# Normalised linear attention with a two-product channel mix: batch 0's first tile handled alone

## The chip, the cores and the metric

The kernel runs on one core of a Trainium2 chip. The metric is device time in microseconds (us). Engines are named as in the profile: PE (TensorE, matmuls), PEld (its weight loads), DVE (VectorE), ACT (ScalarE), POOL (GpSimd, which issues most loads here) and SP (SyncE, which issues the stores).

## The reference

```python
kv  = einsum('bhsd,bhse->bhde', k, v)              # q, k, v: 8 x 8 x 576 x 64
o   = einsum('bhsd,bhde->bhse', q, kv)
x   = o / sqrt(mean(o*o, -1) + 1e-6) * g_norm      # per head, then heads side by side: 8 x 576 x 512
xn  = (x - mean(x)) / sqrt(var(x) + 1e-6) * g_ln   # over the 512
out = x + relu(xn @ w_ch1) @ w_ch2                 # 512 -> 2048 -> 512
```

## The kernel before, in words

A batch has 576 rows; they are worked as four tiles of 128 rows and a remainder of 64, and the remainders of two batches share a tile. For a batch: kv per head pair on PE, q turned (so that d lies on the partitions), then for each tile `o` (q times kv, four matmuls), squares on ACT (`sq`), sums on DVE (`red`), the root on ACT (`root`), its reciprocal on DVE (`inv`), and x from it. `xc` is x less its mean, times g_ln, in bf16; it is turned (`turn`, or `half_turn`/`halves_turn` for 256 columns at a time) into `xT`. The first product (`mm1`, L402) multiplies w1 with `xT`, and ACT takes it through relu (L405); the second (`mm2`, `mm2_part`, L418) multiplies with w2; `finish` (L423) scales by 1/std, adds x and stores.

There are two ways to x. Later tiles use `y` and `x` (two DVE passes over o: times the reciprocal, times g_norm). Batch 0's tiles 0 and 1 use `o_g` and `x_g`: four more matmuls with kv already times g_norm (`kv_g`), and one DVE pass.

The order is written by hand. Every group of 16 matmuls of the first product, and every four of the second, calls `tick()`, which first runs what the agenda holds for that slot (`at(slot, fn)`). Each engine executes its instructions in the order in which they were recorded, so what is recorded earlier on an engine stands ahead. PSUM buffers come from the pools `ps_m` (1), `ps_out` (2), `ps1` (3) and `ps2` (2).

Batch 0 is the start-up, and the place of the change. k comes by the SP and ACT queues, everything else by POOL's: v in two halves, q's lower rows in two halves of the heads, w1's first quarter, q's upper rows, the rest of w1, w2, then batch 1. PE first runs 18 filling matmuls on zeros (`fill`, L196; nobody reads their result). `kv_first` makes kv for two head pairs at a time and copies it to `kv_pack` and, times g_norm, to `kv_g`. Then tiles 0 and 1 go together, by halves of the heads: `half_turn` turns q of both tiles, `half_o` makes o and its squares, `half_red` the sums. Filling matmuls stand in the waits. Tile 0's `xT` is turned before the first product starts; tile 1's, q of tiles 2 and 3 and of the remainder (`turn_first`) and tiles 2 and 3 are on the agenda. The first product of batch 0 runs tile by tile, columns 0 to 8 of tile 0 (in units of 128, four to a group), then 0 to 8 of tile 1, and so on; its second product accumulates the first 8 of 16 for all four tiles, then 8 more for each, and finishes each.

Lines: kv's matmuls L219, their copies L222 and L223, times g_norm L224 and L225; q's turn L183, its copy L191 (tiles 2, 3, remainder) or L492 (tiles 0, 1); o L500 (by halves) and L260, squares L502 and L266, sums L506 and L287, root L297, reciprocal L304; `o_g` L272, `x_g` L278; `xc` by halves L532, its turn L541 and copy L542, whole L321, turn L337 and copy L339; q of batch 1 regrouped L590.

Of the kernel before, what the change touches and what calls it, by code (L numbers as in the profile page):

```python
# [14 lines left out]
def kernel(  # L15
# [11 lines left out]
    nc = tc.nc  # L27
    f32 = mybir.dt.float32
    bf16 = mybir.dt.bfloat16
# [56 lines left out]
    def lo(t, b, h0=0, h1=H):  # L86
        return t[b, h0:h1, :S_LO, :].rearrange("h (p j) d -> p h j d", j=JJ)
# [29 lines left out]
    def pairs(t, hp0, hp1):  # L117
        return bass.AP(tensor=t.tensor, offset=t.offset + hp0 * 2 * S * D,
                       ap=[[JP * D, 128], [2 * S * D, hp1 - hp0], [1, JP * D]])
# [3 lines left out]
    nc.vector.memset(fill_sb, 0.0)  # L123
    nc.sync.dma_start(k_f[:, :HP // 2], pairs(k, 0, HP // 2))
    nc.scalar.dma_start(k_f[:, HP // 2:], pairs(k, HP // 2, HP))
    nc.gpsimd.dma_start(v_p[:, :HP // 2], pairs(v, 0, HP // 2))  # L126
    nc.gpsimd.dma_start(v_p[:, HP // 2:], pairs(v, HP // 2, HP))
    for h0 in (0, H // 2):
        nc.gpsimd.dma_start(q_in[0][:64, h0:h0 + H // 2], lo(q, 0, h0, h0 + H // 2))
    load_w1(0)  # L130
    make_identity(nc, identity)
    nc.gpsimd.dma_start(q_in[0][64:, :, :J], up(q, 0))
# [44 lines left out]
    def turn_groups(tp, i, h0, h1):  # L177
        groups = ((0, 2 * i), (0, 2 * i + 1)) if i < 2 else ((64, 2 * i - 4), (64, 2 * i - 3))
        if i == J:
            groups = ((0, J),)  # L180
        for h in range(h0, h1):
            for half, (p0, j) in enumerate(groups):
                nc.tensor.transpose(  # L183
                    tp[h % 2 * D:h % 2 * D + D, (h - h0) // 2, half * 64:half * 64 + 64],
                    q_in[0][p0:p0 + 64, h, j, :], identity[p0:p0 + 64, p0:p0 + 64])
        return 64 * len(groups)

    def turn_first(i, pool, tag, copy=nc.scalar.copy):
        tp = pool.tile([128, HP, 128], bf16, tag=tag, name="tp")
        n = turn_groups(tp, i, 0, H)  # L190
        copy(qts[0][:, i, :, :n], tp[:, :, :n])  # L191

    def fill(n, pool=ps2, tag="p2"):
        for _ in range(n):
            p1 = pool.tile([128, 512], f32, tag=tag, name="p1")
            nc.tensor.matmul(p1, lhsT=fill_sb[:, :128], rhs=fill_sb, start=True, stop=True)  # L196
            del p1

    def turn_q_dma(b):
        q_p = kv_in.tile([128, JJ, H, D], bf16, tag="qp", bufs=2)  # L200
# [3 lines left out]
            q_t.rearrange("p j hp t -> p (j hp) t"), q_p.rearrange("p j h d -> p (j h d)"))  # L204
        qts[b] = q_t

    def kv_first():
        kvp = held[0] = kv_pack[0]
        g = g_norm_sb.to_broadcast([128, HP // 2, D])
        for i, (pe, te, po, to) in enumerate(((ps_m, "misc", ps1, "p1"), (ps1, "p1", ps1, "p1"))):  # L210
            even = pe.tile([128, HP // 2, D], f32, tag=te, name="even")
            odd = po.tile([128, HP // 2, D], f32, tag=to, name="odd")
            hps = slice(i * HP // 2, (i + 1) * HP // 2)
            for hp in range(hps.start, hps.stop):
                for j in range(JP):
                    js = slice(j * D, (j + 1) * D)
                    for hh, dst in ((0, even), (1, odd)):
                        rows = slice(hh * D, hh * D + D)
                        nc.tensor.matmul(dst[rows, hp - hps.start, :], lhsT=k_p[rows, hp, js],  # L219
                                         rhs=v_p[rows, hp, js],  # L220
                                         start=(j == 0), stop=(j == JP - 1))
            nc.vector.tensor_copy(kvp[:D, hps, :D], even[:D])  # L222
            nc.scalar.copy(kvp[D:, hps, D:], odd[D:])  # L223
            nc.vector.tensor_mul(kv_g[:D, hps, :D], even[:D], g[:D])  # L224
            nc.vector.tensor_mul(kv_g[D:, hps, D:], odd[D:], g[D:])  # L225
            del even, odd

    def kv_of(b):
        kv_ps = ps_m.tile([128, HP, D], f32, tag="misc", name="kv_ps")
# [114 lines left out]
    def main_tile(b, j, pool=None, tag="ops"):  # L344
        q_t, kvp = qts[b], held[b]
        if b not in blks:
            blks[b] = new_block("main", 3)
        return Tile([(slice(0, 128), lambda hp: q_t[:, j, hp, :], kvp)], blks[b], j, pool, tag)
# [109 lines left out]
    def at(slot, fn):  # L458
        agenda.setdefault(int(slot), []).append((slot, fn))
# [12 lines left out]
    del gl_row  # L472

    qts[0] = qt_pool.tile([128, JJ, HP, 128], bf16, tag="qt", name="qt")
    fill(18)
    kv_first()


    t = [main_tile(0, i, ps2, "p2") for i in range(4)]
    for i in range(2):  # L480
        t[i].ss = work.tile([128, H, 1], f32, tag="ss", bufs=4, name="ss")
    sqs = [work.tile([128, H, D], f32, tag="sq", name="sq") for _ in range(2)]
    banks = (((ps_out, "ops"), (ps_m, "misc")), ((ps_out, "ops"), (ps1, "p1")))
    copies = ((nc.scalar.copy, nc.scalar.copy), (nc.vector.tensor_copy, nc.vector.tensor_copy))

    def half_turn(half):
        hp0 = half * HP // 2
        tps = [ps2.tile([128, HP // 2, 128], bf16, tag="p2", name="tp") for _ in range(2)]
        for i in range(2):
            turn_groups(tps[i], i, 2 * hp0, 2 * hp0 + H // 2)  # L490
        for i in range(2):
            copies[half][i](qts[0][:, i, hp0:hp0 + HP // 2], tps[i])  # L492

    def half_o(i, half):
        hp0 = half * HP // 2
        pool, tag = banks[half][i]
        o = pool.tile([128, H // 2, D], f32, tag=tag, name="o_half")
        flat = o.rearrange("p h e -> p (h e)")
        for k2 in range(HP // 2):
            nc.tensor.matmul(flat[:, k2 * 128:(k2 + 1) * 128], lhsT=qts[0][:, i, hp0 + k2, :],  # L500
                             rhs=kv_pack[0][:, hp0 + k2, :], start=True, stop=True)
        nc.scalar.activation(sqs[i][:, half * H // 2:(half + 1) * H // 2], o, func=AF.Square)  # L502

    def half_red(i, half):
        hs = slice(half * H // 2, (half + 1) * H // 2)
        nc.vector.tensor_reduce(t[i].ss[:, hs], sqs[i][:, hs], axis=AX.X, op=ALU.add)  # L506

    half_turn(0)
    fill(2, ps_out, "ops")
    half_o(0, 0)  # L510
    half_turn(1)
    half_o(1, 0)
    half_o(0, 1)
    half_red(0, 0)
    half_red(0, 1)
    half_o(1, 1)
    t[0].root()
    half_red(1, 0)
    half_red(1, 1)
    t[0].o_g(ps1, "p1")  # L520
    t[1].o_g(ps1, "p1")
    fill(8)
    t[0].x_g()
    t[1].root()


    def halves_xc(i):
        x_blk, st, _ = t[i].blk
        for c in range(2):
            cs = slice(c * Dm // 2, (c + 1) * Dm // 2)  # L530
            xc = work.tile([128, Dm // 2], bf16, tag="xch", bufs=4, name="xc")
            nc.vector.scalar_tensor_tensor(xc, in0=x_blk[:, i, cs], scalar=st[:, 1, i:i + 1],  # L532
                                           in1=g_ln_sb[:, cs], op0=ALU.add, op1=ALU.mult)
            yield xc

    def halves_turn(i, xcs, pool, tag):
        xT = t[i].blk[2]
        for c, xc in enumerate(xcs):
            tp = pool.tile([128, 2, 128], bf16, tag=tag, name="tp")
            for kk in range(2):  # L540
                nc.tensor.transpose(tp[:, kk, :], xc[:, kk * 128:(kk + 1) * 128], identity)  # L541
            nc.scalar.copy(xT[:, 2 * c:2 * c + 2, i * 128:(i + 1) * 128], tp)  # L542

    halves_turn(0, halves_xc(0), ps_out, "ops")
    t[1].x_g()
    xc1 = list(halves_xc(1))


    def x2():
        t[2].red()  # L550
        t[2].y()
        t[2].x()
        t[2].xc()

    def x3():
        t[3].sq()
        t[3].red()
        t[3].y()
        t[3].x()
        t[3].xc()  # L560

    def o2():
        t[2].o()
        t[2].sq()

    def next_loads():
        nc.gpsimd.memset(k_in[0][64:, :, J], 0.0)
        nc.gpsimd.memset(v_in[0][64:, :, J], 0.0)
        load_batch(2)

    at(1, lambda: turn_first(2, ps_m, "misc", nc.vector.tensor_copy))
    at(1.1, lambda: halves_turn(1, xc1, ps_out, "ops"))
    at(1.2, o2)
    at(1.3, x2)
    at(4, lambda: turn_first(3, ps_m, "misc"))
    at(5, lambda: t[3].o())
    at(5.1, x3)
    at(6, lambda: t[2].turn(True))
    at(9, lambda: turn_first(J, ps_m, "misc"))
    at(9.5, next_loads)  # L580
    at(10, lambda: t[3].turn(True))
    for i in range(4):
        at(16 + i, lambda i=i: t[i].var())
    at(20, lambda: (rstd_of(0), t.clear()))
# [41 lines left out]
    at(32 * B + 14, lambda: rstd_of("rem"))  # L626


    for ts, c0, c1 in ((0, 0, 8), (1, 0, 8), (0, 8, 12), (1, 8, 12), (0, 12, 16), (1, 12, 16),
                       (2, 0, 16), (3, 0, 16)):  # L630
        mm1(0, ts, 1, c0, c1)
    p2s = [ps1.tile([128, Dm], f32, tag="p1", name="p2") for _ in range(2)]
    p2s += [ps2.tile([128, Dm], f32, tag="p2", name="p2") for _ in range(2)]
    for ts in range(4):
        mm2_part(0, ts, p2s[ts], 0, nDe // 2)
    for ts in range(4):
        p2 = p2s[ts]
        p2s[ts] = None
        mm2_part(0, ts, p2, nDe // 2, nDe)
        finish(0, ts, p2)  # L640
        del p2
    del blks[0], m1s[0]
# [41 lines left out]
```

## Time and profile before

| | |
|---|---|
| median of 5 runs | 291.66 us (291.62 to 291.71) |
| the profiled execution | 291.63 us, of which the span 289.5 us |
| PE busy | 282.0 us, 97% of the span |
| DVE, ACT busy | 151.0 and 155.0 us |
| L402, first product | 1024 matmuls, 131.8 us |
| L418, second product | 608 matmuls, 129.2 us |
| L196, filling matmuls | 28, 8.2 us |
| v's two halves | 288 KB each, 6.5 us from issue to landing (median) |
| q's two lower halves | 160 KB each, 7.0 us |

The span runs from the first to the last instruction of the profiled execution; the device time also holds what lies around it. Loads convert from 4-byte to 2-byte numbers on the way, and sizes are those written. Matmuls are pipelined and their ends are modelled, so the busy time of a stretch says whether PE had something to do, not how fast it went; the distance between starts says that. The page has the span in 40 slices of 7.2 us.

### The profile page before, as it was taken

The page shows a single profiled execution, that of the slowest core. Times are in us where ns is not written, and L with a number is a line of the kernel's source. Part 1 is how long each engine was busy: PE and PEld are TensorE (multiplying, and loading weights), DVE is VectorE, ACT ScalarE, POOL GpSimd, SP SyncE. Part 2 cuts the span into 40 slices and gives each one's busy share as a digit, 9 for nine tenths or more (in the row PEclk, how much of TensorE's full clock was granted, in tenths as well). Part 3 has the DMA queues.
Part 4 walks back from the last instruction along what each step waited for, and adds up shares of the span by engine and source line. Part 5 has one row for each costly group of instructions (what it writes and reads, how often), then busy time and mean ns, then how long its engine had stood idle before and what let it go on. Part 6 is the DMA issues. An engine that isn't in the chain of part 4 may idle for free.

```text
span 289.5 us, 5791 instructions
## 1 busy us (share of the span) xinstructions
PE 282.0 (97%) x2312; PEld 158.7 (55%) x2312; DVE 151.0 (52%) x335; ACT 155.0 (54%) x339; POOL 41.1 (14%) x68
## 2 busy tenths in 40 slices
PE   7889999999999999999999999999999999999995
PEld 3579755995569644445444444444444444444444
DVE  5775028847997783765366925762578300220022
ACT  3467755885469832882189418920894076016500
POOL 8522520032032003200410023000000000000000
PEclk9999999999999999999999999999999999999999
DMA  7999999469899919995997189937302510131033
GB/s 214 203 206 204 198 204 219 109 99 196 149 178 144 165 40 156 209 169 100 144 204 110 41 147 197 175 76 149 69 18 54 112 36 0 39 81 28 0 74 73
DMA packets 64378, 36.10 MB, mean 125 GB/s; under 512 B 31836, under 2 KB 59356, under 8 KB 64352
## 3 DMA queue, kind: packets, MB, share of 16 engines
q0 software_dynamic: 28016, 17.76, 44.2%
q1 hardware_dynamic: 35824, 17.25, 31.1%
q10 hardware_dynamic: 512, 0.72, 0.8%
q8 instruction: 18, 0.29, 0.4%
q14 instruction: 8, 0.07, 0.1%
HBM read 36.71 MB, written 9.44 MB: 159 GB/s over the span
## 4 chain that ended last, share of the span: by engine, by line
PE 93%; DMA 2%; ACT 1%; DVE 1%; issue 1%; POOL 0%; POOLq 0%
PE p L418 43%; PE p L402 43%; PE o_ps L260 3%; DMA v_in<-in_v_dram 2%; PE kv_ps L235 2%; PE tp L183 1%; PE p L196 1%; PE tp L337 1%; ACT sq L266 0%; PE tp L170 0%; DVE xc L532 0%; PE o_half L500 0%; POOL v_in L126 0%; ACT m L405 0%; DVE x_blk L278 0%
## 5 line engine op out<-in xcount | busy, mean ns | idle before, releaser
L402 PE MATMUL p<-xT_blk,w_sb 128*128 128x128 bf16 (+2 forms) x1024 | 131.8, 286 | 0.2
L418 PE MATMUL p<-w_sb,m 128*128 128x512 bf16 (+2 forms) x608 | 129.2, 368 | 0.0
L405 ACT ACTIVATE m<-p 128x512 bf16<-128x512 f32 x144 | 85.5, 596 | 43.3 <-PE p L402 41.1
L402 PEld LDWEIGHTS <-w_sb 128*128 128x128 bf16 x1024 | 78.4, 98 | 44.1 <-issue 0.6
L418 PEld LDWEIGHTS <-m 128*128 128x128 bf16 x608 | 56.8, 98 | 61.7
L423 DVE SCALAR_TENSOR_TENSOR o_sb<-p,rstd,x_blk 128x512 f32<-128x512 f32 (+2 forms) x38 | 27.4, 721 | 54.3 <-PE p L418 51.4
L266 ACT ACTIVATE sq<-o_ps 128x512 f32<-128x512 f32 x34 | 20.2, 595 | 41.5 <-PE o_ps L260 41.4
L287 DVE TENSOR_REDUCE ss<-sq 128x8 f32<-128x512 f32 x34 | 23.0, 678 | 11.2 <-ACT sq L266 11.2
L329 ACT ACTIVATE dev<-x_blk,st_blk 128x512 f32<-128x512 f32 x36 | 25.7, 714 | 4.6 <-DVE st_blk L315 4.4
L321 DVE SCALAR_TENSOR_TENSOR xc<-x_blk,st_blk,g_ln_sb 128x512 bf16<-128x512 f32 x34 | 25.6, 752 | 1.2
L292 DVE TENSOR_TENSOR y<-o_ps,inv 128x512 f32<-128x512 f32 x34 | 23.5, 692 | 3.0
L311 DVE SCALAR_TENSOR_TENSOR x_blk<-y,g_norm_sb 128x512 f32<-128x512 f32 x34 | 23.5, 692 | 1.2
L411 DVE RECIPROCAL rstd<-rstd 128x4 f32<-128x4 f32 x9 | 1.6, 174 | 35.3 <-ACT rstd L410 35.3
L304 DVE RECIPROCAL inv<-rms 128x8 f32<-128x8 f32 x36 | 7.2, 200 | 23.0 <-ACT rms L297 23.0
L98 POOL COPY gate<-qt 1x1 bf16<-1x1 bf16 x5 | 0.9, 177 | 114.1 <-DMA qt<-q_p 114.1
L297 ACT ACTIVATE rms<-ss,eps_sb 128x8 f32<-128x8 f32 x36 | 10.7, 297 | 9.4 <-DVE ss L287 8.7
L260 PEld LDWEIGHTS <-qt 128*128 128x128 bf16 (+1 forms) x152 | 9.9, 100 | 7.4 <-issue 1.7
L260 PE MATMUL o_ps<-kv_pack,qt 128*128 128x128 bf16 (+1 forms) x152 | 13.3, 220 | 0.2 <-DVE qt L191 0.2
L196 PE MATMUL p<-fill_sb 128*128 128x512 bf16 x28 | 8.2, 451 | 1.2 <-DVE eps_sb L137 1.2
L329 ACT ACTIVATION_READ_ACCUMULATOR dev<-x_blk,st_blk 128x1 f32 x36 | 6.9, 191 | 0.0
L238 ACT CAST kv_pack<-kv_ps 64x256 bf16<-64x256 f32 x7 | 2.6, 366 | 7.2 <-PE kv_ps L235 7.2
L235 PEld LDWEIGHTS <-k_in 128*64 128x64 bf16 x280 | 5.0, 112 | 2.6 <-issue 2.5
(79 smaller groups left out, 117.0 us busy)
## 6 DMA issues: line engine op xcount, KB each, us to landing
out_dram<-o_sb SPq DMA_DIRECT2D x70, 128.0 KB, 2.5
w_sb<-in_moe_w_ch_dram POOLq DMA_DIRECT2D x8, 512.0 KB, 13.9
k_in<-in_k_dram POOLq DMA_DIRECT2D x7, 320.0 KB, 6.0
v_in<-in_v_dram POOLq DMA_DIRECT2D x7, 320.0 KB, 9.1
q_in<-in_q_dram POOLq DMA_DIRECT2D x7, 320.0 KB, 13.0
q_in<-in_q_dram POOLq DMA_DIRECT2D x8, 256.0 KB, 12.8
k_in<-in_k_dram POOLq DMA_DIRECT2D x7, 256.0 KB, 6.9
v_in<-in_v_dram POOLq DMA_DIRECT2D x7, 256.0 KB, 11.2
```

The source lines that it names most:

```text
L196: nc.tensor.matmul(p1, lhsT=fill_sb[:, :128], rhs=fill_sb, start=True, stop=True)
L260: nc.tensor.matmul(flat[rows, hp * 128:(hp + 1) * 128], lhsT=lhsT_of(hp), rhs=kvp[:, hp, :], start=True, stop=True)
L266: nc.scalar.activation(self.sq_t, self.o_ps, func=AF.Square)
L287: nc.vector.tensor_reduce(self.ss, self.sq_t, axis=AX.X, op=ALU.add)
L292: nc.vector.tensor_mul(self.y_t, self.o_ps, self.inv().to_broadcast([128, H, D]))
L311: nc.vector.scalar_tensor_tensor(x_blk[:, ts].rearrange("p (h d) -> p h d", h=H), in0=self.y_t, scalar=1.0, in1=g_norm_sb.to_broadcast([12 ...
L321: nc.vector.scalar_tensor_tensor(self.xc_t, in0=x_blk[:, self.ts], scalar=st[:, 1, self.ts:self.ts + 1], in1=g_ln_sb, op0=ALU.add, op1=ALU ...
L329: nc.scalar.activation(dev, x_blk[:, ts], func=AF.Square, bias=st[:, 1, ts:ts + 1], accum_out=st[:, 2, ts:ts + 1])
L402: nc.tensor.matmul(p1[:, i, :], lhsT=w1_sb[:, kk, de * 128:(de + 1) * 128], rhs=blk[2][:, kk, sl], start=(kk == 0), stop=(kk == nK - 1))
L405: nc.scalar.activation(m1[:, de0:de0 + per, sl], p1, func=AF.Relu)
L418: nc.tensor.matmul(p2[:, c0:c1], lhsT=m1s[b][:, de, ts * 128:(ts + 1) * 128], rhs=w2_sb[:, de, c0:c1], start=(de == 0), stop=(de == nDe - 1))
L423: nc.vector.scalar_tensor_tensor(o_sb[:, c0:c1], in0=p2[:, c0:c1], scalar=rstds[b][:, ts:ts + 1], in1=blks[b][0][:, ts, c0:c1], op0=ALU.mu ...
```

## The change

It is confined to batch 0, in six places.

- Loads: v's first three head pairs in one piece, then of q's lower rows the first two of five columns (all that tile 0 needs), then v's last pair, then the rest of q's lower rows. Before: v's two halves, then two halves of q by heads.
- kv in parts of three pairs and of one (`KvFirst`), each with its copies and its products with g_norm placed one by one. Tile 0's q is turned between the two parts, whole.
- Tile 0 alone: its o, squares and sums in two parts (six heads and two). Tile 1's o, squares and sums follow whole, its sums behind tile 0's two `xc` halves; its q, and the remainder's, are turned within the first wait.
- On slot 1 q of tiles 2 and 3 is turned one right behind the other, around them tile 1's `xT` halves (the second one copied by DVE instead of ACT) and tile 2's o; tile 2 takes the way by `o_g` and `x_g`. Tile 3's o is on slot 5 as before, `turn` of tile 2 on 5 instead of 6, of tile 3 on 11 instead of 10.
- The first product of batch 0 runs tiles 0 and 1 by turns, four columns at a time, so that tile 1 is needed by the second group; tile 2's first 12 stand before columns 12 to 16 of all. The second product accumulates 8, 4 and 4 of 16, each for all four tiles, and finishes each in the last round.
- Filling matmuls write one buffer over and over (`fill(n, p1)`) and so don't wait for each other; 18 at the start as before, then 1, 3 and 5 instead of 2 and 8.

```diff
-    nc.gpsimd.dma_start(v_p[:, :HP // 2], pairs(v, 0, HP // 2))
-    nc.gpsimd.dma_start(v_p[:, HP // 2:], pairs(v, HP // 2, HP))
-    for h0 in (0, H // 2):
-        nc.gpsimd.dma_start(q_in[0][:64, h0:h0 + H // 2], lo(q, 0, h0, h0 + H // 2))
+    nc.gpsimd.dma_start(v_p[:, :HP - 1], pairs(v, 0, HP - 1))
+    nc.gpsimd.dma_start(q_in[0][:64, :, :2], lo(q, 0)[:, :, :2])
+    nc.gpsimd.dma_start(v_p[:, HP - 1:], pairs(v, HP - 1, HP))
+    nc.gpsimd.dma_start(q_in[0][:64, :, 2:], lo(q, 0)[:, :, 2:])
...
+    kv_a = KvFirst(0, HP - 1, ((ps_m, "misc"), (ps1, "p1")))
+    kv_b = KvFirst(HP - 1, HP, ((ps1, "p1"), (ps1, "p1")))
...
+    kv_a.mms()
+    kv_a.copies()
+    turn_first(0, ps2, "p2")
+    kv_a.times_g()
+    fill(1)
+    kv_b.mms()
+    kv_b.copies()
+    part_o(kv_a)
+    part_o(kv_b)
+    part_sq(kv_a)
+    part_sq(kv_b)
+    kv_b.times_g()
+    part_red(kv_a)
+    part_red(kv_b)
+    turn_first(1, ps_m, "misc")
     t[0].root()
-    half_red(1, 0)
-    half_red(1, 1)
-    t[0].o_g(ps1, "p1")
+    t[0].o_g(ps2, "p2")
+    dead = fill(3)
+    t[1].o()
+    t[1].sq()
+    turn_first(J, ps_m, "misc")
     t[1].o_g(ps1, "p1")
-    fill(8)
+    fill(5, dead)
     t[0].x_g()
-    t[1].root()
...
+    for c, xc in enumerate(halves_xc(0)):
+        half_turn(0, c, xc, nc.scalar.copy)
+    t[1].red()
     t[1].x_g()
     xc1 = list(halves_xc(1))
...
+    def before_1():
+        turn_first(2, ps_m, "misc")
+        tp = ps2.tile([128, HP, 128], bf16, tag="p2", name="tp")
+        turn_groups(tp, 3, 0, H)
+        half_turn(1, 0, xc1[0], nc.scalar.copy)
+        t[2].o()
+        half_turn(1, 1, xc1[1], nc.vector.tensor_copy)
+        t[2].sq()
+        nc.scalar.copy(qts[0][:, 3], tp)
+        t[2].red()
+        t[2].root()
+
+    def before_2():
+        t[2].o_g(ps2, "p2")
+        t[2].x_g()
+        t[2].xc()
+
+    def before_5():
+        t[3].o()
+        t[3].sq()
+        t[3].red()
+        t[3].y()
+        t[3].x()
+        t[3].xc()
...
-    for ts, c0, c1 in ((0, 0, 8), (1, 0, 8), (0, 8, 12), (1, 8, 12), (0, 12, 16), (1, 12, 16),
-                       (2, 0, 16), (3, 0, 16)):
+    for ts, c0, c1 in ((0, 0, 4), (1, 0, 4), (0, 4, 8), (1, 4, 8), (0, 8, 12), (1, 8, 12),
+                       (2, 0, 12), (0, 12, 16), (1, 12, 16), (2, 12, 16), (3, 0, 16)):
         mm1(0, ts, 1, c0, c1)
...
-    for ts in range(4):
-        mm2_part(0, ts, p2s[ts], 0, nDe // 2)
+    for de0, de1 in ((0, nDe // 2), (nDe // 2, nDe * 3 // 4)):
+        for ts in range(4):
+            mm2_part(0, ts, p2s[ts], de0, de1)
     for ts in range(4):
...
-        mm2_part(0, ts, p2, nDe // 2, nDe)
+        mm2_part(0, ts, p2, nDe * 3 // 4, nDe)
         finish(0, ts, p2)
```

More of the change, by code (lines that the diff above doesn't have):

```diff
@@ L191, in turn_first, with fill @@
         copy(qts[0][:, i, :, :n], tp[:, :, :n])
-    def fill(n, pool=ps2, tag="p2"):
+    def fill(n, p1=None):
+        if p1 is None:
+            p1 = ps2.tile([128, 512], f32, tag="p2", name="p1")
         for _ in range(n):
-            p1 = pool.tile([128, 512], f32, tag=tag, name="p1")
             nc.tensor.matmul(p1, lhsT=fill_sb[:, :128], rhs=fill_sb, start=True, stop=True)
-            del p1
+        return p1
     def turn_q_dma(b):
@@ L205, in turn_q_dma, with __init__, mms, copies @@
         qts[b] = q_t
[L207 to L214, printed above, removed]
+    class KvFirst:
+        def __init__(self, hp0, hp1, pools):
+            self.hps, self.pools = slice(hp0, hp1), pools
+        def mms(self):
+            n = self.hps.stop - self.hps.start
+            (pe, te), (po, to) = self.pools
+            self.even = pe.tile([128, n, D], f32, tag=te, name="even")
+            self.odd = po.tile([128, n, D], f32, tag=to, name="odd")
+            for hp in range(self.hps.start, self.hps.stop):
                 for j in range(JP):
                     js = slice(j * D, (j + 1) * D)
-                    for hh, dst in ((0, even), (1, odd)):
+                    for hh, dst in ((0, self.even), (1, self.odd)):
                         rows = slice(hh * D, hh * D + D)
-                        nc.tensor.matmul(dst[rows, hp - hps.start, :], lhsT=k_p[rows, hp, js],
-                                         rhs=v_p[rows, hp, js],
+                        nc.tensor.matmul(dst[rows, hp - self.hps.start, :],
+                                         lhsT=k_p[rows, hp, js], rhs=v_p[rows, hp, js],
                                          start=(j == 0), stop=(j == JP - 1))
[L222 to L226, printed above, removed]
+        def copies(self):
+            nc.vector.tensor_copy(kv_pack[0][:D, self.hps, :D], self.even[:D])
+            nc.scalar.copy(kv_pack[0][D:, self.hps, D:], self.odd[D:])
+        def times_g(self):
+            g = g_norm_sb.to_broadcast([128, self.hps.stop - self.hps.start, D])
+            nc.vector.tensor_mul(kv_g[:D, self.hps, :D], self.even[:D], g[:D])
+            nc.vector.tensor_mul(kv_g[D:, self.hps, D:], self.odd[D:], g[D:])
+            del self.even, self.odd
     def kv_of(b):
@@ L474 @@
     qts[0] = qt_pool.tile([128, JJ, HP, 128], bf16, tag="qt", name="qt")
+    held[0] = kv_pack[0]
     fill(18)
[L476 to L516, printed above, removed]
-    t[0].root()
-    half_red(1, 0)
-    half_red(1, 1)
-    t[0].o_g(ps1, "p1")
+    kv_a = KvFirst(0, HP - 1, ((ps_m, "misc"), (ps1, "p1")))
+    kv_b = KvFirst(HP - 1, HP, ((ps1, "p1"), (ps1, "p1")))
@@ new lines, with part_o @@
+    t = [main_tile(0, 0)] + [main_tile(0, i, *((ps1, "p1") if i == 1 else (ps2, "p2")))
+                             for i in range(1, 4)]
+    t[0].ss = work.tile([128, H, 1], f32, tag="ss", bufs=4, name="ss")
+    sq_0 = work.tile([128, H, D], f32, tag="sq", name="sq")
+    o_0 = {}
+    def part_o(kv_x):
+        hp0, hp1 = kv_x.hps.start, kv_x.hps.stop
+        o_0[hp0] = ps_out.tile([128, 2 * (hp1 - hp0), D], f32, tag="ops", name="o_part")
+        flat = o_0[hp0].rearrange("p h e -> p (h e)")
+        for hp in range(hp0, hp1):
+            nc.tensor.matmul(flat[:, (hp - hp0) * 128:(hp - hp0 + 1) * 128],
+                             lhsT=qts[0][:, 0, hp, :], rhs=kv_pack[0][:, hp, :],
+                             start=True, stop=True)
@@ new lines, in part_sq, with part_red @@
+    def part_sq(kv_x):
+        hp0, hp1 = kv_x.hps.start, kv_x.hps.stop
+        nc.scalar.activation(sq_0[:, 2 * hp0:2 * hp1], o_0.pop(hp0), func=AF.Square)
+    def part_red(kv_x):
+        hs = slice(2 * kv_x.hps.start, 2 * kv_x.hps.stop)
+        nc.vector.tensor_reduce(t[0].ss[:, hs], sq_0[:, hs], axis=AX.X, op=ALU.add)
+    kv_a.mms()
[8 more added lines that the diff above has]
+    part_sq(kv_a)
@@ L521 @@
+    part_sq(kv_b)
[3 more added lines that the diff above has]
+    turn_first(1, ps_m, "misc")
+    t[0].root()
+    t[0].o_g(ps2, "p2")
[3 more added lines that the diff above has]
+    turn_first(J, ps_m, "misc")
     t[1].o_g(ps1, "p1")
-    fill(8)
+    fill(5, dead)
+    del dead
     t[0].x_g()
-    t[1].root()
     def halves_xc(i):
@@ L534, in halves_xc, with half_turn @@
             yield xc
[L536 to L544, printed above, removed]
+    def half_turn(i, c, xc, copy):
+        tp = ps_out.tile([128, 2, 128], bf16, tag="ops", name="tp")
+        for kk in range(2):
+            nc.tensor.transpose(tp[:, kk, :], xc[:, kk * 128:(kk + 1) * 128], identity)
+        copy(t[i].blk[2][:, 2 * c:2 * c + 2, i * 128:(i + 1) * 128], tp)
+    for c, xc in enumerate(halves_xc(0)):
+        half_turn(0, c, xc, nc.scalar.copy)
+    t[1].red()
     t[1].x_g()
     xc1 = list(halves_xc(1))
-    def x2():
-        t[2].red()
-        t[2].y()
-        t[2].x()
+    def before_1():
[7 more added lines that the diff above has]
+        nc.scalar.copy(qts[0][:, 3], tp)
+        t[2].red()
+        t[2].root()
+        del tp, xc1[:]
+    def before_2():
+        t[2].o_g(ps2, "p2")
+        t[2].x_g()
         t[2].xc()
-    def x3():
+    def before_5():
+        t[3].o()
         t[3].sq()
@@ L560, in x3 @@
         t[3].xc()
-    def o2():
-        t[2].o()
-        t[2].sq()
     def next_loads():
@@ L569, in next_loads @@
         load_batch(2)
[L571 to L579, printed above, removed]
+    at(1, before_1)
+    at(2, before_2)
+    at(5, lambda: t[2].turn(True))
+    at(5.1, before_5)
     at(9.5, next_loads)
-    at(10, lambda: t[3].turn(True))
+    at(11, lambda: t[3].turn(True))
     for i in range(4):
```

## The prediction, made before the result was known

> **What bounds the kernel now.** I read the page's span in slices first, then the chain that ended last, then the timeline of each engine from 7 to 34 us, then the landings of the first loads.
>
> ```profile
> PE   7889999999999999999999999999999999999995
> ...
> PEclk9999999999999999999999999999999999999999
> ...
> PE 93%; DMA 2%; ACT 1%; DVE 1%; issue 1%; POOL 0%; POOLq 0%
> ```
>
> TensorE is full but for the first three slices (22 us) and the last, and its granted clock is full throughout. So the time is the moment from which TensorE is fed, plus its work, plus the holes in it. The stretches say where the holes are (columns: length, then busy us with counts for PE, PEld, DVE, ACT, POOL, then clock, DMA share, GB/s):
>
> ```profile
> 8.00:16.00 8.00, 6.23 (x119) 3.65 (x112) 6.37 (x21) 3.86 (x12) 3.58 (x6) 1.00 1.30 203
> ...
> 26.00:34.00 8.00, 8.00 (x140) 7.50 (x137) 1.23 (x4) 5.95 (x13) 4.41 (x7) 1.00 1.38 199
> 34.00:50.00 16.00, 15.94 (x137) 8.31 (x136) 7.06 (x15) 9.58 (x25) 2.42 (x3) 1.00 1.34 207
> ```
>
> The change touches what lies before 33 us, and the order of batch 0's second product. TensorE's timeline there (start, us, operation; L402 is the first product, 16 matmuls a group; L183 turns q, L541 and L337 turn x, L260 is q times kv):
>
> ```profile
> 14.94 0.68 PE L541 MATMUL tp<-identity,xc 128*128 128x128 bf16 x4 [0.84 <-DVE xc L532]
> 15.69 1.34 PE L402 MATMUL p<-xT_blk,w_sb 128*128 128x128 bf16 x16
> 16.96 0.44 PE L183 MATMUL tp<-identity,q_in 64*64 64x64 bf16 x16
> 17.33 0.40 PE L541 MATMUL tp<-identity,xc 128*128 128x128 bf16 x4
> 17.93 0.40 PE L260 MATMUL o_ps<-kv_pack,qt 128*128 128x128 bf16 x4 [0.20 <-DVE qt L191]
> 18.16 2.84 PE L402 MATMUL p<-xT_blk,w_sb 128*128 128x128 bf16 x48
> ...
> 27.92 5.52 PE L402 MATMUL p<-xT_blk,w_sb 128*128 128x128 bf16 x96
> 33.28 1.03 PE L418 MATMUL p<-w_sb,m 128*128 128x512 bf16 x4
> ```
>
> The first group that counts starts at 15.69 and waits for its third matmul until 16.09. From 18.16 on, 15 groups, 24 q transposes, 8 x transposes and 4 o matmuls fill the time to 33.28. Unit prices from these rows: a group 0.893 (96 matmuls run 27.92 to 33.28), 16 q transposes 0.37, four 128-wide matmuls 0.22. Later work is as many matmuls as before, so the forecast is: when does batch 0's second product (L418) start instead of 33.28?
>
> What sets 15.69 is tile 0's chain, on VectorE and ScalarE:
>
> ```profile
> 12.64 0.30 ACT L297 ACTIVATE rms<-ss,eps_sb 128x8 f32<-128x8 f32 x1 [0.21 <-DVE ss L506]
> 13.18 0.19 DVE L304 RECIPROCAL inv<-rms 128x8 f32<-128x8 f32 x1
> 13.48 0.69 DVE L278 SCALAR_TENSOR_TENSOR x_blk<-og_ps,inv 128x512 f32<-128x512 f32 x1
> ```
>
> VectorE is doing tile 1's sums (L506, 12.19 to 13.2) when tile 0's root is ready at 12.94. That is what handling tile 0 alone removes.
>
> **The change, step by step** (estimates of the new kernel in us from the span's start, each from a row of before).
>
> *Loads.* v's halves (288 KB, 256 packets of 1152 bytes each) landed at 7.45 and 8.89, q's halves (160 KB, 256 of 640 bytes) at 9.68 and 10.5. The software queue moved no packet before 5.6, when k was done, and ran without a hole since, so the order of the four issues decides and their issue time (2.9 us together, as before) does not. Price per packet: 1152 bytes 5.6 ns, 1024 bytes 4.9 (w1), 640 bytes 3.2, 512 bytes 2.6 (q's upper rows: 512 packets, 12.95 to 14.29). The new q pieces have 512 packets of 256 and of 384 bytes, which the trace does not show. Bounds: in proportion to bytes 0.67 and 1.0 us; at the 512-byte price 1.34 each. The line through the four rows gives 1.5 and 2.1 ns, so 0.78 and 1.07, which I take. Landings: three pairs of v 7.45 + 0.72 = 8.17; q's first piece 8.95; v's last pair 9.67; rest of q 10.75. Everything behind is 0.25 later: w1's first quarter 13.2 and q's upper rows 15.45, needed at 14.9 and 16.2, so covered; beyond that cover it is one for one.
>
> [...]
>
> *Tile 0.* kv's matmuls follow their landing by 0.08 (rows 0.09, 0.04) and each other by 0.016: 54 from 8.25 to 9.10. Copies begin 0.21 later, as at 8.31 before. The turn of tile 0 starts at 9.12 (its q is there); ScalarE's copy follows at 9.66, behind the kv copy, 0.58 long: 10.24. v's last pair: 18 matmuls 9.75 to 10.03, copied by 10.46, behind VectorE's two products with g. o: 10.33; squares from 10.70 (128x384, 0.49, between the rows for 256 and 512) and 11.12; sums 0.55 and 0.29 wide from 11.26, overlapping 0.09 as the rows do: 12.01. Root 12.04, reciprocal 12.38, x 12.68 against 13.48: **-0.80**. ScalarE's copy of tile 1's q stands ahead of that root: turn at 10.8, copy 11.36 to 11.94, so it just fits.
>
> *First group.* x to third matmul was 13.48 to 16.09; the same 2.61 gives 15.29, and the group ends at 17.03 - 0.80 = 16.23. The nine new filling matmuls (ten before) end at 13.8, and the turn of the 64-row remainder and tile 1's o stand in the same wait, so they cost nothing while x's transpose comes at 14.14.
>
> *Tile 1.* Here time is given back. Its sum now follows both halves of tile 0's xc: 14.42 to 15.11; the root waits for ScalarE's xT copies: 15.18; reciprocal 15.52; x at 15.82 against 15.51. So tile 1 is 0.31 later while tile 0 is 0.80 earlier, and the second group needs tile 1, where before it needed tile 0 alone: the cover is gone. TensorE: q of tiles 2 and 3 (0.74) to 16.97; hole of 0.31 until x's first half (15.82 + 1.46 = 17.28); o of tile 2 at 17.43, behind relu and copy on ScalarE; second half 17.68; ScalarE's xT copy done 17.98, VectorE's (0.28 as L492's) 18.29. Group two: two matmuls at 18.0, the rest from 18.34, to 19.21 (0.87 as in group one). Holes together 0.82.
>
> *From there.* 14 groups 12.50, og of tile 2 0.22 (new; it replaces one VectorE pass of 0.69), x of tiles 2 and 3 and o of tile 3 0.66. One hole: tile 3's root stands on ScalarE ahead of a relu, and the fourth group behind needs that buffer: 0.1, where before lost 0.3 to the same at 25.4. Sum 13.48: the second product begins at 32.69, against 33.28: **-0.59**.
>
> *Second product in 8, 4, 4 instead of 8, 8.* Same matmuls. Its four finishes move together behind ticks 28 to 31. VectorE runs nearly without a hole from 44.3 to 57.2 there; it ends tile (1,2)'s xc at 55.87 and TensorE takes it at 56.96. I get 56.1 in the new order: cost nothing by 0.3 to 0.8; without that cover, one for one.
>
> The profiled execution was 291.63 (span 289.5 and 2.1 around it; the median of five is 291.66). 291.63 - 0.59 = **291.0**.
>
> [...]
>
> **Rivals.**
> 1. *More gain.* If tile 1's chain is a few tenths earlier than my row sums, the holes of 0.82 close for the most part: -1.2, 290.4. For: every hole has the same cause. Against: the VectorE order is fixed, its durations are rows.
> 2. *The gain goes back.* Tile 1's x at 16.4 instead of 15.82 (its sum or root pushed behind a copy) moves group two one for one: 291.6. For: three engines alternate with no slack there.
> 3. *Slower.* Tile 1's q copy stands ahead of tile 0's root on ScalarE, and the last q piece lands last. Landing later than about 11.0 delays the root one for one (turn, copy and hand-over take 1.04 to the root at 12.04), and q's first piece delays the turn as well. If a packet of 256 or 384 bytes costs what one of 640 does (3.2 ns), the pieces take 1.66 each: turn 0.75 later, rest of q at 12.2, x at 13.95, +0.68: 292.3. The gain is gone from about 2.6 ns a packet on, which is the 512-byte price. Against: the four rows lie on one line.
> 4. *Not as it says.* If v's last pair is late anyway, tile 0 alone waits for it in o; that is inside the sum (VectorE, not the landing, sets 10.46).
>
> **Numbers.** Forecast 0.55, rival 1 0.16, rival 2 (with 4) 0.12, rival 3 0.17. 0.2% is 0.58 us, about what a measurement of this kernel can tell from no change. The forecast lies on that edge: of its 0.55 I give 0.34 to faster. Faster 0.34 + 0.16 = 0.50; within 0.21 + 0.12 = 0.33; slower 0.17. The forecast's own range is 290.7 to 291.4. Range for all 290.3 to 292.3: from rival 1 to rival 3 at the 640-byte price.
>
> **What would show it.** Right: x of tile 0 near 12.7, first group near 14.9, holes before and inside group two, second product near 32.7. Wrong: q's first piece landing after 9.5, tile 0's root waiting for a copy, tile 1's x after 16.4, TensorE waiting for a relu between 22 and 28 or for xc near 57, or a clock below 1.00.

## The result, and the profile after

| | before | after |
|---|---|---|
| median | 291.74 us (50 runs) | 290.92 us (26 runs, 290.78 to 292.71) |
| ratio, 95% interval | | 0.9969 [0.9961, 0.9976] |
| the profiled execution | 291.63 us | 290.97 us |
| its span | 289.5 us | 289.2 us |
| outside the span | 2.13 us | 1.77 us |
| batch 0's second product begins | 33.28 us | 32.98 us |

The kernel is faster by 0.31%, and 291.0 was forecast. The table holds a warning, though: the span became shorter by 0.30 us only, where the prediction had 0.59, and 0.36 us went from a part of the time that the prediction did not speak of. (One of the 26 executions, 292.71, has a mean clock of 0.994; the last section says what that may be.)

Lines of the new kernel: q's turn L183, kv L224, o L502 and L270, `o_g` L282, `x_g` L288, `xc` by halves L546, its turn by halves L553 and whole L347, copies of the whole turn L349, first product L412, relu L415, second product L428, root L307, reciprocal L314, fill L197.

The page of after, its slices (tenths busy) and its chain by engine:

```profile
PE   8889999999999999999999999999999999999995
...
PEclk9999999999999999999999999999999999999999
...
PE 91%; DMA 2%; DVE 2%; ACT 2%; issue 1%; DVEq 0%; POOLq 0%
```

At this scale only the first digit and two points of the chain have changed. The stretches of after (same columns as before):

```profile
8.00:16.00 8.00, 7.24 (x155) 4.87 (x155) 5.67 (x18) 4.37 (x12) 3.75 (x6) 1.00 1.35 202
...
26.00:34.00 8.00, 7.96 (x130) 7.31 (x128) 1.55 (x4) 5.81 (x11) 4.45 (x7) 1.00 1.38 199
```

PE is busy a microsecond more between 8 and 16 us, with 155 matmuls instead of 119, but between 26 and 34 it issues 130 where it issued 140 before. Most of these ten are another mix (before has eight turns of q there, and after is 0.30 further into the second product, whose matmuls are longer), so the count says where to look, not what is lost. The timeline of PE in after (start, us, operation) shows the gain and where it is given back:

```profile
14.20 0.68 PE L553 MATMUL tp<-identity,xc 128*128 128x128 bf16 x4
14.95 1.34 PE L412 MATMUL p<-xT_blk,w_sb 128*128 128x128 bf16 x16
16.21 0.70 PE L183 MATMUL tp<-identity,q_in 64*64 64x64 bf16 x32
17.30 0.28 PE L553 MATMUL tp<-identity,xc 128*128 128x128 bf16 x2 [0.39 <-DVE xc L546]
...
18.05 1.26 PE L412 MATMUL p<-xT_blk,w_sb 128*128 128x128 bf16 x16
19.14 0.39 PE L282 MATMUL og_ps<-kv_g,qt 128*128 128x128 bf16 x4
...
22.49 5.76 PE L412 MATMUL p<-xT_blk,w_sb 128*128 128x128 bf16 x96
28.09 0.39 PE L347 MATMUL tp<-identity,xc 128*128 128x128 bf16 x4
28.31 4.83 PE L412 MATMUL p<-xT_blk,w_sb 128*128 128x128 bf16 x80
32.98 1.24 PE L428 MATMUL p<-w_sb,m 128*128 128x512 bf16 x5
```

The first group ends at 16.21 instead of 17.03: -0.82. Then there is the wait for tile 1 at 17.30, and one inside the second group (16 matmuls in 1.09 between the starts at 18.05 and 19.14, where 0.89 is the price). The two long pieces of the first product take too long as well, and the bracket shows nothing of it, because PE's busy time is modelled through such holes; the distance of starts does: 96 matmuls 22.49 to 28.09 are 5.60 (price 5.36), 80 matmuls 28.31 to 32.98 are 4.67 (price 4.47). What stands in these two, the chain of waits of after tells (start, us, what):

```profile
24.57 0.30 ACT rms L307
24.88 0.49 ACT m L415
...
25.41 2.85 PE p L412 x48
28.29 0.60 ACT m L415
28.88 0.49 ACT xT_blk L349
...
29.41 3.73 PE p L412 x64
```

At 24.57 tile 3's root runs on ScalarE ahead of a relu, and PE waits for the buffer that this relu empties. At 28.88 the copy of tile 3's turned `xc` has had to wait for a relu, and the matmuls that read it start at 29.41: only one group covers the way from turn to copy. The first of these is in the prediction (0.1 was written, 0.24 it is); the second (0.20) is not.

### The profile page after: what moved, and what is told of

It reads as the page before. It is cut to its first block, busy times and chain, and to the rows that moved or that the text cites. A ratio compares the mean times of both kernels' runs of the same rounds, so it can differ in the third digit from the quotient of the medians.

```text
span 289.2 us, 5791 instructions
## 1 busy us (share of the span) xinstructions
PE 282.3 (98%) x2315; PEld 158.9 (55%) x2315; DVE 149.8 (52%) x331; ACT 155.5 (54%) x338; POOL 41.0 (14%) x68
## 4 chain that ended last, share of the span: by engine, by line
PE 91%; DMA 2%; DVE 2%; ACT 2%; issue 1%; DVEq 0%; POOLq 0%
PE p L428 43%; PE p L412 42%; PE o_ps L270 3%; DMA v_in<-in_v_dram 2%; PE kv_ps L245 2%; ACT m L415 1%; DVE x_blk L288 0%; DVE xc L546 0%; PE tp L347 0%; ACT sq L276 0%; ACT xT_blk L349 0%; PE tp L170 0%; ACT rms L307 0%; DVE ss L512 0%; PE odd L224 0%
## 5 line engine op out<-in xcount | busy, mean ns | idle before, releaser
L412 PE MATMUL p<-xT_blk,w_sb 128*128 128x128 bf16 (+2 forms) x1024 | 131.8, 286 | 0.4
L428 PE MATMUL p<-w_sb,m 128*128 128x512 bf16 (+2 forms) x608 | 129.2, 368 | 0.0
L415 ACT ACTIVATE m<-p 128x512 bf16<-128x512 f32 x144 | 85.5, 596 | 43.8 <-PE p L412 41.8
L412 PEld LDWEIGHTS <-w_sb 128*128 128x128 bf16 x1024 | 78.5, 98 | 44.6 <-issue 1.1
L428 PEld LDWEIGHTS <-m 128*128 128x128 bf16 x608 | 56.8, 98 | 61.7
L276 ACT ACTIVATE sq<-o_ps 128x512 f32<-128x512 f32 x35 | 20.8, 596 | 42.1 <-PE o_ps L270 42.1
L297 DVE TENSOR_REDUCE ss<-sq 128x8 f32<-128x512 f32 x35 | 23.7, 678 | 11.4 <-ACT sq L276 11.4
L302 DVE TENSOR_TENSOR y<-o_ps,inv 128x512 f32<-128x512 f32 x33 | 22.8, 692 | 3.0
L321 DVE SCALAR_TENSOR_TENSOR x_blk<-y,g_norm_sb 128x512 f32<-128x512 f32 x33 | 22.8, 692 | 1.1
L314 DVE RECIPROCAL inv<-rms 128x8 f32<-128x8 f32 x36 | 7.2, 201 | 24.8 <-ACT rms L307 24.8
L307 ACT ACTIVATE rms<-ss,eps_sb 128x8 f32<-128x8 f32 x36 | 10.7, 297 | 8.0 <-DVE ss L297 7.7
L270 PEld LDWEIGHTS <-qt 128*128 128x128 bf16 (+1 forms) x156 | 10.2, 100 | 7.3 <-issue 1.7
L270 PE MATMUL o_ps<-kv_pack,qt 128*128 128x128 bf16 (+1 forms) x156 | 13.7, 220 | 0.0
L197 PE MATMUL p<-fill_sb 128*128 128x512 bf16 x27 | 8.5, 467 | 1.2 <-DVE eps_sb L137 1.2
```

What stands on the lines that cost most here:

```text
L270: nc.tensor.matmul(flat[rows, hp * 128:(hp + 1) * 128], lhsT=lhsT_of(hp), rhs=kvp[:, hp, :], start=True, stop=True)
L276: nc.scalar.activation(self.sq_t, self.o_ps, func=AF.Square)
L297: nc.vector.tensor_reduce(self.ss, self.sq_t, axis=AX.X, op=ALU.add)
L302: nc.vector.tensor_mul(self.y_t, self.o_ps, self.inv().to_broadcast([128, H, D]))
L321: nc.vector.scalar_tensor_tensor(x_blk[:, ts].rearrange("p (h d) -> p h d", h=H), in0=self.y_t, scalar=1.0, in1=g_norm_sb.to_broadcast([12 ...
L412: nc.tensor.matmul(p1[:, i, :], lhsT=w1_sb[:, kk, de * 128:(de + 1) * 128], rhs=blk[2][:, kk, sl], start=(kk == 0), stop=(kk == nK - 1))
```

## The experiments

The theory after the result: PE's way through the start-up is the predicted one but for two holes that were sized wrongly or missed, and the 0.36 outside the span is the program's and has nothing to do with it. Its rival on the second point: the time outside is a thing of the chip or the day, and the kernel before would show the smaller value too if it were run beside. On the first point each hole has a rival of its own: that it belongs to something else and stays when its supposed cause is taken away. What each would give is in the expectation of each run. So the kernel before was run again, and parts of the change were taken back, or a hole's cause removed, one at a time. Differences from after are between medians; the median of before itself lay between 291.64 and 291.74 in the different sets of runs, so about 0.1 us of such a difference means nothing.

**before_again**: the kernel before, unchanged.

> The kernel before once more, to see where the time outside the span differs. In the two profiles the spans differ by 0.3 us (289.5 and 289.2), the profiled executions by 0.66 (291.63 and 290.97), the medians by 0.82. Theory 1, the single profiled execution of before had a short span by chance: its other executions show spans near 289.9 with about 1.8 us around them, and the change is worth some 0.7 inside the span. Theory 2, something outside the span became shorter: spans near 289.5 with 2.1 to 2.2 around them, and only 0.3 of the gain is what the changed order did.

Measured: 291.64 us (10 runs), ratio 0.9995 [0.9983, 1.0008]; span about 289.5, and in each execution of this kernel 2.09 to 2.21 us outside the span. After and every variant of it have 1.72 to 1.85. So the 0.36 comes from the program, and the rival on this point falls.

**q_behind**: the two loads in the middle change places; q's first piece comes behind v's last pair.

```diff
-    nc.gpsimd.dma_start(q_in[0][:64, :, :2], lo(q, 0)[:, :, :2])
     nc.gpsimd.dma_start(v_p[:, HP - 1:], pairs(v, HP - 1, HP))
+    nc.gpsimd.dma_start(q_in[0][:64, :, :2], lo(q, 0)[:, :, :2])
```

> The changed kernel with q's first piece behind v's last pair again (both pieces in their new cut). Theory, the landing of what tile 0's turn needs sets its chain: q's first piece lands at about 9.65 instead of 9.0, the turn starts at 9.7 instead of 9.13, x of tile 0 at 13.3 instead of 12.73, the first group 0.55 later and the time +0.5. Rival, kv's second part sets it (its copies end at 10.65 in the changed kernel and VectorE is what they wait for): v's last pair is there 0.75 earlier, the copies of part two move ahead, and the time changes by less than 0.2.

Measured: 291.38 (11 runs), ratio 0.9987 [0.9978, 0.9996], 0.46 above after. PE's timeline of this kernel has the wait at the turn:

```profile
9.62 0.44 PE L183 MATMUL tp<-identity,q_in 64*64 64x64 bf16 x16 [0.46 <-DMA q_in<-in_q_dram]
```

The turn moves from 9.13 to 9.62, the first group from 14.95 to 15.30, the second product from 32.98 to 33.34. Of the 0.49 by which the turn is later, 0.36 reaches the second product (0.46 between the medians, where +0.5 was expected). So a late q does delay what is behind it, as rival 3 says; only its price per packet was not reached.

**loads_old**: after, with the four loads of before.

```diff
-    nc.gpsimd.dma_start(v_p[:, :HP - 1], pairs(v, 0, HP - 1))
-    nc.gpsimd.dma_start(q_in[0][:64, :, :2], lo(q, 0)[:, :, :2])
...
+    nc.gpsimd.dma_start(v_p[:, :HP // 2], pairs(v, 0, HP // 2))
+    nc.gpsimd.dma_start(v_p[:, HP // 2:], pairs(v, HP // 2, HP))
+    for h0 in (0, H // 2):
+        nc.gpsimd.dma_start(q_in[0][:64, h0:h0 + H // 2], lo(q, 0, h0, h0 + H // 2))
```

> The changed kernel with v and q loaded in halves as before. Theory, tile 0 alone is worth nothing without its loads: kv's first part waits for v's second half (8.9), the turn of tile 0 for q's second half (10.5 instead of 9.0), and the whole front is 1.4 later, tile 1 with it: time about +1.3 against the changed kernel, so slower than before. Rival, what was recorded earlier on each engine (one tile at a time) is the gain and the loads add a few tenths: +0.3 to +0.6. The time outside the span: 2.15 if the loads are its cause, 1.78 if not.

Measured: 293.68 (6 runs), ratio 1.006 [1.0042, 1.0077]. One execution kept the full clock: 292.23, 1.3 above after. The others took 293.2 to 294.1 at a mean clock of 0.994. In the profiled one (columns as in the stretches above, the clock third from the end):

```profile
8.00:10.00 2.00, 0.96 (x49) 0.74 (x42) 0.63 (x3) 0.25 (x1) 1.25 (x2) 1.00 1.31 198
10.00:12.00 2.00, 1.19 (x31) 0.82 (x33) 0.69 (x3) 0.58 (x2) 1.59 (x3) 0.95 1.25 207
12.00:14.00 2.00, 2.00 (x39) 1.61 (x34) 1.33 (x5) 1.39 (x5) 0.29 (x2) 0.50 1.37 198
14.00:16.00 2.00, 2.00 (x21) 1.05 (x19) 1.45 (x6) 0.83 (x3) 1.12 (x2) 0.70 1.25 210
```

PE was busy 2.15 of 4 us from 8 to 12 and then ran at a clock of 0.50, by the clock column from 11.8 to 15.2. So the new order on the engines, without its loads, is slower than before: the turn has to wait for both halves of q (at the full clock 292.23, against 291.71 for before beside it), and in five of six executions the clock fell as well. The rest of the change gains nothing without the order of the loads. What the new loads alone would give to the kernel before was not run.

**no_fill**: the nine unread matmuls in the waits left out (the 18 at the start stay).

```diff
-    fill(1)
...
-    dead = fill(3)
...
-    fill(5, dead)
-    del dead
```

> The changed kernel without the nine unread matmuls in the waits (1, 3 and 5); the 18 at the start stay. Leaves out no part of the computation. Theory, they only fill waits: tile 0's x and the first group at the same times within 0.05, time the same within 0.15. Rival, they hold the clock up: the granted clock falls below 1 in the stretch 10 to 20, the first groups take up to twice 0.89, time +0.5 to +1.5.

Measured: 293.13 (12 runs, 291.65 to 295.15), ratio 1.0052 [1.0031, 1.0072]; mean clock of the executions 0.977 to 0.994, never full. The profiled one:

```profile
12.00:14.00 2.00, 0.76 (x16) 0.45 (x14) 1.60 (x6) 1.05 (x3) 0.52 (x1) 1.00 1.36 199
14.00:16.00 2.00, 1.70 (x15) 1.29 (x16) 1.50 (x4) 0.94 (x3) 0.24 (x2) 0.80 1.26 207
16.00:18.00 2.00, 2.00 (x42) 1.57 (x39) 1.37 (x5) 1.17 (x2) 0.60 (x1) 0.50 1.24 206
18.00:20.00 2.00, 1.73 (x24) 1.58 (x24) 0.98 (x2) 1.45 (x3) 0.68 (x1) 0.85 1.24 206
```

PE busy 0.76 of 2 us between 12 and 14 (after: 2.00), and then a clock of 0.50, by the clock column from 15.2 to 18.6. Tile 0's turn is not later (14.00), so the fills delay nothing; the first group takes 1.95 from start to start (14.75 to 16.70) where after takes 1.26. The nine matmuls that nobody reads are worth 2.2 us between the medians, more than the whole change.

**before_fill**: the kernel before, its fills writing one buffer.

```diff
+        p1 = pool.tile([128, 512], f32, tag=tag, name="p1")
         for _ in range(n):
-            p1 = pool.tile([128, 512], f32, tag=tag, name="p1")
...
-            del p1
+        del p1
```

> The kernel before with its 28 filling matmuls written as in the changed kernel: each of the three stretches writes one buffer, so that none waits for the one before. Two questions. First, the time outside the span is 2.13 to 2.17 us in every execution of before and 1.75 to 1.82 in every one of the changed kernel and its variants, also in the one without the nine filling matmuls: if the fills' waits and buffers are its cause, it is 1.8 here and the time -0.35; if not, 2.15 and the time unchanged. Second, before has executions at up to 293 with a granted clock of 0.994: if closer fills hold the clock better, these become fewer.

Measured: 291.69 (11 runs), ratio 1.0001 [0.9992, 1.001], 2.11 to 2.19 outside the span. How the fills use buffers gains nothing, and is not the 0.36. The second question stays open: in this set of runs neither kernel has an execution at 0.994.

**mm1_two**: the first product's order of before (two groups of tile 0, then two of tile 1).

```diff
-    for ts, c0, c1 in ((0, 0, 4), (1, 0, 4), (0, 4, 8), (1, 4, 8), (0, 8, 12), (1, 8, 12),
+    for ts, c0, c1 in ((0, 0, 8), (1, 0, 8), (0, 8, 12), (1, 8, 12),
```

> The changed kernel with columns 0 to 8 of tile 0 first, then 0 to 8 of tile 1, so that the second group needs tile 0 alone as before. Theory, group two waits for tile 1's xT copies: without them it starts when its weights are there; w1's second quarter landed at 17.76 in the changed kernel, so at about 17.85 to 18.0 in one piece, and the hole before its third matmul (18.1 to 18.36) is gone: time -0.2 to -0.4. Rival, the weights are the limit and land late: no change, or slower by what they are late.

Measured: 290.64 (5 runs), ratio 0.9959 [0.9943, 0.9974], 0.28 below after. The second group's rows on PE's timeline of this kernel:

```profile
17.91 1.07 PE L412 MATMUL p<-xT_blk,w_sb 128*128 128x128 bf16 x16
18.81 0.39 PE L282 MATMUL og_ps<-kv_g,qt 128*128 128x128 bf16 x4
```

The second group starts without waiting for tile 1's copies and has no hole (0.90). From the first group to the second product PE takes 17.64 us (15.01 to 32.65), where after takes 18.03. The wait ahead of tile 1's turn stays (0.40), since that turn stands ahead of this group on PE in both orders.

**root3_later**: tile 3's `y`, `x` and `xc` are recorded on slot 6 instead of 5, so that its root stands behind one more relu.

```diff
+    def before_6():
         t[3].y()
         t[3].x()
         t[3].xc()
...
+    at(6, before_6)
```

> The changed kernel with tile 3's y, x and xc (and with them its root on ScalarE) recorded one slot later. In the changed kernel that root (24.57) waits for tile 3's sum with the relu of group 6 behind it (24.78), and TensorE's 96 matmuls from 22.49 take 5.60 to the next turn instead of 5.36. Theory, the relu kept behind the root holds a PSUM buffer that the third group behind needs: the hole of 0.24 goes, tile 3's turn comes at about 27.85 if its xc (ready at 27.6) is not later, time -0.15 to -0.25. Rival, the hole comes from tile 2's xT copy: time unchanged.

Measured: 290.63 (5 runs), ratio 0.9963 [0.995, 0.9977], 0.29 below after. On PE's timeline of this kernel

```profile
22.52 5.52 PE L412 MATMUL p<-xT_blk,w_sb 128*128 128x128 bf16 x96
27.88 0.39 PE L347 MATMUL tp<-identity,xc 128*128 128x128 bf16 x4
```

the 96 matmuls take 5.36: the hole of 0.24 is gone.

**xt3_dve**: VectorE copies tile 3's turned `xc`, instead of ScalarE.

```diff
-    at(11, lambda: t[3].turn(True))
+    at(11, lambda: t[3].turn(True, nc.vector.tensor_copy))
```

> The changed kernel with tile 3's xT copied by VectorE instead of ScalarE. In the changed kernel one group stands between tile 3's turn (28.09) and the first group that needs it, and ScalarE's copy (28.78 to 29.36) stands behind a relu; 80 matmuls take 4.67 to the second product instead of 4.47. Theory, that is the hole which the prediction did not have: the copy moves to about 28.5 to 28.95, the hole of 0.2 goes, time -0.2. Rival, it lies elsewhere in those five groups: unchanged.

Measured: 290.65 (5 runs), ratio 0.9967 [0.9954, 0.9979], 0.27 below after. The 80 matmuls run from 28.20 to 32.66, 4.46: the hole of 0.20 is gone. VectorE has room there: 1.55 us busy of 8 between 26 and 34 in after.

**three**: the last three edits together.

> All three together: columns 0 to 8 of tile 0 and then of tile 1, tile 3's root one slot later, tile 3's xT by VectorE. If the three holes are separate, their gains add: -0.28 (as measured for the first) -0.2 -0.2, so about 0.65 to 0.7 faster than the changed kernel, 290.2 us. If a later wait takes their place (tile 3's xc, which then is needed earlier), half of that.

Measured: 290.24 (5 runs, 290.19 to 290.31), ratio 0.9951 [0.9938, 0.9963], span 288.5. On its PE timeline

```profile
17.95 1.07 PE L412 MATMUL p<-xT_blk,w_sb 128*128 128x128 bf16 x16
...
22.20 5.52 PE L412 MATMUL p<-xT_blk,w_sb 128*128 128x128 bf16 x96
27.56 0.39 PE L347 MATMUL tp<-identity,xc 128*128 128x128 bf16 x4
27.79 4.63 PE L412 MATMUL p<-xT_blk,w_sb 128*128 128x128 bf16 x80
32.25 2.11 PE L428 MATMUL p<-w_sb,m 128*128 128x512 bf16 x8
```

the holes in the group and in the two long pieces are gone, but they do not simply add. The second product begins 0.73 earlier than in after, yet 0.17 of that is an earlier front in this execution (its first group starts at 14.78, after's at 14.95). From the first group to the second product it takes 17.47 us, 0.56 less than after, where the three edits alone saved 0.39, 0.22 and 0.20 (17.64, 17.81 and 17.83). What is missing stands before the second group: it starts 0.42 behind the turn ahead of it (17.53 to 17.95), where in mm1_two it starts 0.14 behind (17.77 to 17.91). Its weights, w1's second quarter, landed at 17.81 in after. That the group waits for them here fits the rival which mm1_two's expectation named; the landing in this execution was not shown. Between medians this version is 0.68 below after, where the three differences add to 0.84; that 0.65 to 0.7 was forecast is partly luck. It beats both kernels.

**mm2_two**: the second product of batch 0 in 8 and 8 as before.

```diff
-    for de0, de1 in ((0, nDe // 2), (nDe // 2, nDe * 3 // 4)):
+    for de0, de1 in ((0, nDe // 2),):
...
-        mm2_part(0, ts, p2, nDe * 3 // 4, nDe)
+        mm2_part(0, ts, p2, nDe // 2, nDe)
```

> The changed kernel with batch 0's second product in 8 and 8 of 16 again, as before. The prediction costed this edit at nothing, with VectorE's finishes as the cover. Theory: time and span within 0.1 of the changed kernel. It also asks for the time outside the span (1.78 with the change, 2.15 without): 2.15 here if the order of these matmuls and finishes is its cause, and the time then +0.35.

Measured: 290.82 (7 runs), ratio 0.997 [0.9959, 0.998], 1.74 to 1.82 outside: 0.10 below after, no more than the medians of before differ among themselves. The split gains nothing that these runs could show.

**t2_y**: tile 2 by `y` and `x` again.

```diff
-        t[2].o_g(ps2, "p2")
-        t[2].x_g()
+        t[2].y()
+        t[2].x()
```

> The changed kernel with tile 2's x by two VectorE passes (y, x) instead of o_g and x_g. The sum had four matmuls more for it (0.22) and one VectorE pass of 0.69 less. Theory, TensorE gains 0.22 and then waits for tile 2's xc: it was ready at 21.57 and taken at 22.05; now 22.3 against 21.83, so a hole of about 0.45, net +0.2 to +0.3 and the gain of the four matmuls more than lost. Rival, the cover is enough: -0.2.

Measured: 290.98 (9 runs), ratio 0.9974 [0.9965, 0.9983]: 0.06 above after, where +0.2 to +0.3 was expected: a miss. Its PE timeline

```profile
22.20 0.40 PE L347 MATMUL tp<-identity,xc 128*128 128x128 bf16 x4 [0.29 <-DVE xc L331]
...
22.66 5.52 PE L412 MATMUL p<-xT_blk,w_sb 128*128 128x128 bf16 x96
```

has the expected hole before tile 2's turn (0.29; 0.45 was expected), but PE is spared four matmuls (0.22), and the 96 run in 5.36: they start later (22.66 instead of 22.49), and PE no longer waits for the buffer behind tile 3's root. A hole was traded for another one and for work.

## Why the prediction came out, point by point

- **Loads: right.** Landings forecast 8.17, 8.95, 9.67 and 10.75; by the semaphores of after they are 8.29, 9.06, 9.74 and 10.75. The two new pieces took 0.77 and 1.01 us, forecast 0.78 and 1.07. (The first packet of the software queue, which the prediction puts at 5.6, moved at 5.36 in the trace of before; nothing in the sum hangs on it.) A packet of 256 bytes took 41 ns on its engine and one of 384 bytes 51 (640: 69; 1152: 107): on the line through the larger ones. Rival 3 needed more.
- **Tile 0: right, to 0.05.** On the timeline of all engines of after

```profile
12.08 0.30 ACT L307 ACTIVATE rms<-ss,eps_sb 128x8 f32<-128x8 f32 x1
12.41 0.20 DVE L314 RECIPROCAL inv<-rms 128x8 f32<-128x8 f32 x1 [0.37 <-ACT rms L307]
12.73 0.69 DVE L288 SCALAR_TENSOR_TENSOR x_blk<-og_ps,inv 128x512 f32<-128x512 f32 x1
```

  (forecast 12.04, 12.38, 12.68). VectorE is free when the root comes; x is 0.75 earlier than in before.
- **First group and tile 1: right.** The group ends at 16.21 (16.23); tile 1's x at 15.84 (15.82), its first turn 17.30 (17.28), the third matmul of the second group 18.36 (18.34). The time is given back where the prediction says; mm1_two shows that the hole inside the group (1.09 instead of 0.89) is due to the order by turns.
- **From there on: the step that failed.** "One hole: tile 3's root stands on ScalarE ahead of a relu [...]: 0.1" is 0.24 (root3_later), and there is a second hole of 0.20 (xt3_dve) that the prediction does not have: its sum has no term for `turn` of tile 3 on slot 11 instead of 10, and it did not ask what covers the copy. With the smaller differences these make 32.98 out of 32.69. The span gained 0.30, not 0.59.
- **The sum: right by luck, through two errors that cancel.** "291.63 - 0.59 = 291.0" takes the 2.1 us around the span as constant. They fell to 1.77. -0.30 - 0.36 = -0.66 is the measured step. The forecast of the time was good, the account of it only in its first half.
- **Fills "cost nothing": right but incomplete.** They delay nothing. That they are worth 2.2 us was not in the prediction, whose sum has no term for the clock: in this kernel without them it fell to 0.50 for 3.4 us, though the longest idle time of PE after 8.2 us is 1.24.
- **Second product in 8, 4, 4: right**, by mm2_two.
- Rival 1's time, 290.4, is about what "three" reaches (290.24), but by edits, not by a quicker tile 1. Rivals 2 and 4 did not occur.

**Open:** what takes 0.36 us out of the time outside the span. Not a drift of the measurement (before_again), not the fills' buffers (before_fill) or number (no_fill), not the order of the loads, of the first or of the second product, nor tile 2's way to x: each of these kernels has the value of its parent. In both profiles the first load is issued at 0.75 and the first matmul starts at 1.20, and 1.3 us lie between the last packet stored and the end of the span. Not tried one by one: kv in unequal parts, tile 0 alone. So of the 0.66 between the two profiled executions, 0.30 is explained and 0.36 is not.

## What to carry to other kernels

When a start-up chain is shortened, follow the next three or four tiles through the engine that everybody shares (here ScalarE: root, relu, copy): each operation that is now closer to its reader needs its cover counted again, and the distance of starts, not the busy time, shows the hole. Matmuls that nobody reads belong to the price of a wait (nine of them were worth 2.2 us here); take them out only with the granted clock in view. Compare the span and the time around it separately, or two errors may pass for a good account.

## What the runs showed of the hardware that was not expected

- **The clock fell after half-idle stretches.** In no_fill PE had 0.76 busy of 2 us between 12 and 14 and no idle time over 1.24 after 8.2; in loads_old 2.15 of 4 between 8 and 12, with gaps of 0.74, 0.34 and 0.77. Both then had a clock of 0.50 for 3.4 us (15.2 to 18.6, and 11.8 to 15.2). In the 3.4 us before the fall PE was busy 1.86 us (no_fill) and 1.55 us (loads_old), worked out from the rows of 2 us: 55% and 46%. In the profiled executions of before and after, whose clock stayed at 1.00 there, no stretch of that length between 5 and 30 us is busy less than 63% (before, 2.17 of 3.40 from 6.3; after, 2.20 of 3.40 from 7.0). So among these four the busy share tells the two apart, and the length of the longest gap does not (0.77 between 8 and 12 in loads_old, whose clock fell; 1.12 in after, whose clock held).
- **How much of the time is at the low clock differs between executions.** Only the two profiled falls show their length, 3.4 us each. Such a stretch takes 3.4 x 0.5 / 290 = 0.006 off the mean clock. The executions of no_fill stand at 0.992 to 0.994 (291.7 us), 0.987 or 0.988 (292.8 to 293.2), 0.982 (293.7 to 294.2) and 0.977 (295.15), which is one, two, three and four such stretches by that sum, an estimate, at about 1.1 us each; in loads_old one (0.994) cost 1.0 to 1.9. The 292.71 of after, at 0.994, would be one. What makes the number differ no run shows.
- **The start ran at half pace, and the clock row does not say so.** In before and after the 18 filling matmuls start 0.43 us apart at first and 0.22 later. In before they took 5.75 us, in after 6.01, where the change of pace came one matmul later; the profile's clock row is full in both. "Full throughout" in the prediction holds only behind them.
- **Device time outside the span differed with the program**: 2.09 to 2.21 us in the kernel before and before_fill, 1.72 to 1.85 in after and all its variants.
